# Splits on ScalarE, the cluster assignment in PSUM, and a planner with new numbers

## The chip, the cores and the metric

The kernel runs on one core of a Trainium2 chip. The core has five engines that each take their instructions in order: TensorE (PE, with its weight loads PEld), VectorE (DVE), ScalarE (ACT), GpSimd (POOL) and SyncE (SP, which here issues the DMAs). Time is device microseconds, the median of several runs. The profile is of one execution.

## The reference

Attention over 4 batches and 8 heads, 768 tokens, head size 64, in which a query sees only the keys of its own cluster, and then a soft mixture of experts over the result:

```python
q_n = q / (np.linalg.norm(q, axis=-1, keepdims=True) + 1e-06)   # k_n, c_n alike
q_assign = np.argmax(np.einsum('bhsd,hcd->bhsc', q_n, c_n), axis=-1)   # 16 clusters; k_assign alike
mask = q_assign[:, :, :, None] == k_assign[:, :, None, :]
scores = np.where(mask, scale * np.matmul(q, k.transpose(0, 1, 3, 2)), -1000000000.0)
scores = scores - np.max(scores, axis=-1, keepdims=True)
attn = np.exp(scores)
attn = attn / (np.sum(attn, axis=-1, keepdims=True) + 1e-09)
x = np.matmul(attn, v)          # [3072, 512] once the heads are side by side
logits = x @ phi                # 32 slots, 4 for each of 8 experts
slot_input = softmax(logits, over='tokens').T @ x      # written out in the reference
slot_out[e] = np.maximum(slot_input[e] @ w1[e], 0.0) @ w2[e]
out = softmax(logits, over='slots') @ slot_out
```

## The kernel before

Attention works through 32 heads in 16 pairs. For a pair, TensorE multiplies q and k with the centroids (`sims`), ScalarE scales the result (`sims_out`), TensorE transposes it into a PSUM bank (`assign`), and VectorE finds the first largest of 16 similarities for every token (`assign1` to `assign3`, lines 470 to 490): a maximum, a comparison with it into bfloat16 in SBUF, a multiplication with 16, 15, ... 1, another maximum, and two comparisons that write one-hot rows. `onehot` transposes these, and they become 32 more rows of the operands, so that the score product carries the mask.

For a head, q^T and k^T arrive in `R` (three buffers). `split_hi` (line 512) rounds them to the type of TensorE's faster float32 products into `RH`, `split_lo` (line 515) writes what is left into `RL` (two buffers each). DMAs within SBUF (`place1`, `place2`, `place_mask`, `place3`, line 325) lay the pieces and the mask out as operands. `splitv_hi` (line 543, or 541 on ScalarE) and `splitv_lo` (line 547) split v likewise into float16 (`vx`, two buffers). Pass a (line 560) computes scores in nine steps, each into one of two PSUM banks, and VectorE takes the row maxima of each (`rowmax`, line 568). The maxima go back as a row of the operands (`maxrow`, line 583, and a small DMA). Pass b (line 603) computes the transposed scores for six key tiles into two PSUM buffers; ScalarE takes the exponential of each twice (`expo`, line 609: float32 and float16), GpSimd subtracts one from the other (`elow`, line 613), and pass c (line 625) multiplies both parts with v and accumulates. VectorE divides by the sums (`norm`, lines 637 to 639). Transposes and logits of the finished pair follow, and after eight heads the routing of one batch. The experts come after the last head. Forty pieces of expert weights are loaded during the attention, the others into the buffers that the attention leaves.

In the kernel before, `HI_ACT` puts `split_hi` of heads 0 and 1 on ScalarE and the other 30 on VectorE, and `EARLY` does the same with `splitv_hi`.

The order of all this is made by a planner when the kernel is built (`Plan`). Each operation has an engine, an assumed duration, the buffers that it reads and writes, and a priority from the table `K`; the planner simulates the engines and always takes, of the operations that can start first, the one of the lowest number. What it emits is the fixed order of each engine's instructions; the hardware then only follows it and waits on semaphores. A PSUM bank shared by all small products (`pt`, one buffer: `sims`, `assign`, `onehot`, `maxrow`, `xtrans`, `logits` and the routing) is modelled as a token: `get` takes it, `put` returns it.

Of the kernel before, what the change touches and what calls it, by code (L numbers as in the profile page):

```python
# [19 lines left out]
P = 128  # L20
LOOK = 0.0
HI_ACT = lambda i: i < 2 or i % 2 == HA
HA = 2
MX_ACT = False
WARM0 = 60
WARM1 = (0, 4, 3, 2, 4, 1)   # after the last xtrans, xtrans, logits, dtrans, slotin, comb
EARLY = 2              # heads whose first steps keep off the vector engine


class Plan:  # L30
    """Operations in program order, with the buffers that they read and write; order() lets every
# [15 lines left out]
    def op(self, eng, us, key, t, fn, rd=(), wr=(), get=None, put=None, after=(), xfer=0.0):  # L47
# [16 lines left out]
        self.ops.append((eng, us, t + self.K[key], fn, deps, get, put, xfer, key, t))  # L64
# [12 lines left out]
    def order(self, look=LOOK, banks=1):  # L77
# [9 lines left out]
        dma = tail = 0.0  # L87
        gets, puts = [], {}
# [16 lines left out]
        while len(out) < N:  # L105
# [42 lines left out]
def clustered_attention_then_soft_moe(  # L148
    ctx: ExitStack,
    tc: tile.TileContext,  # L150
    qkT: bass.AP,    # [B, H, 2*D, S]    rows 0:D = q^T, rows D: = k^T
    vt: bass.AP,     # [B, H, 128, S/128, D]
    cent: bass.AP,   # [128, H/2, D]   rows (half, head, q|k, cluster), for every pair of heads
    cbdT: bass.AP,   # [2*D, H, 2*NCL] centroids^T for q and for k, zero elsewhere
    phi2: bass.AP,   # [128, DM/128, NS]
    w1r: bass.AP,    # [2, 4, 128, 4, F]
    w2a: bass.AP,    # [2, 2, 128, 4, F/256, DM/2]   first half of the columns
    w2b: bass.AP,    # [2, 2, 128, 4, F/128, DM/4]   the other two quarters
    out: bass.AP,    # [B*S, DM]
# [4 lines left out]
    NT = S // P                  # token tiles of a head  # L164
    HS = S // 2                  # half of the tokens
# [35 lines left out]
    descb = const.tile([P, NCL], BF16, name="descb")  # L201
# [6 lines left out]
    def consts1():  # L208
        nc.vector.tensor_copy(descb, desc)
# [18 lines left out]
    # of the batches so far, rows (quarter of the tokens, slot):  # L228
    # min of -logits, sum of exp, sum of exp * x
# [7 lines left out]
    # Sixteen chunks of expert weights go through NWB buffers; the last of the  # L237
    # buffers hold tiles of the attention first.
# [5 lines left out]
    # two of them are allocated in parts, which change their type when the weights come  # L244
# [49 lines left out]
    # the last columns of the arenas  # L294
# [6 lines left out]
    swp = cols(ar7, A0 + NCC * NS, P)            # adds up the quarters  # L301
# [236 lines left out]
    def splitv_hi(i):  # L538
        o = VXs[i % 2][:, :, D:2 * D]
        if i < EARLY:  # L540
            nc.scalar.mul(o, V[i % 2], VS)  # L541
        else:
            nc.vector.tensor_scalar_mul(o, V[i % 2], VS)  # L543
# [689 lines left out]
```

## Time and profile before

| | |
|---|---|
| median of 3 runs | 562.71 us (562.12 to 568.84) |
| the profiled execution | span 563.4 us; no other time of its own is given, and the span is 0.7 us above the median |
| DVE busy | 465.5 us, 83% of the span |
| PE busy | 478.6 us, 85% |
| ACT busy | 340.2 us, 60% |
| POOL busy | 345.7 us, 61% |
| DMA, mean | 184 GB/s |

Busy time is the union of an engine's instructions. Matmuls overlap and their ends are modelled, so PE's figure holds some drain time as well. The 83% of DVE is a mean over stages: it is higher during the attention, and low in the last 80 us, in which the experts run.

### The profile page before, as it was taken

The page shows a single profiled execution, that of the slowest core. Times are in us where ns is not written, and L with a number is a line of the kernel's source. Part 1 is how long each engine was busy: PE and PEld are TensorE (multiplying, and loading weights), DVE is VectorE, ACT ScalarE, POOL GpSimd, SP SyncE. Part 2 cuts the span into 40 slices and gives each one's busy share as a digit, 9 for nine tenths or more (in the row PEclk, how much of TensorE's full clock was granted, in tenths as well). Part 3 has the DMA queues.
Part 4 walks back from the last instruction along what each step waited for, and adds up shares of the span by engine and source line. Part 5 has one row for each costly group of instructions (what it writes and reads, how often), then busy time and mean ns, then how long its engine had stood idle before and what let it go on. Part 6 is the DMA issues. An engine that isn't in the chain of part 4 may idle for free.

```text
span 563.4 us, 15227 instructions
## 1 busy us (share of the span) xinstructions
PE 478.6 (85%) x6083; PEld 376.8 (67%) x6083; DVE 465.5 (83%) x786; ACT 340.2 (60%) x494; POOL 345.7 (61%) x255
## 2 busy tenths in 40 slices
PE   8896868789888889789888889887988799899994
PEld 6685657577767667667676667776765678764484
DVE  3799698998989998989899998999899988452253
ACT  4176536676667667667676667676765687830142
POOL 7067465777767657777766578676866598714210
PEclk9999878999999999999999999999999899999998
DMA  8824537346656566676666646665765478999978
GB/s 222 216 70 120 152 98 204 102 130 186 172 142 178 147 154 164 178 177 155 169 168 180 155 125 161 181 176 151 174 175 151 132 204 203 308 311 382 408 248 239
DMA packets 55082, 103.79 MB, mean 184 GB/s; under 512 B 8490, under 2 KB 22372, under 8 KB 55012
## 3 DMA queue, kind: packets, MB, share of 16 engines
q1 hardware_dynamic: 55012, 102.82, 65.2%
q8 instruction: 48, 0.79, 0.6%
q14 instruction: 22, 0.18, 0.1%
HBM read 52.76 MB, written 6.29 MB: 105 GB/s over the span
## 4 chain that ended last, share of the span: by engine, by line
DVE 49%; PE 28%; DMA 12%; issue 5%; SPq 3%; ACT 1%; POOL 0%; DVEq 0%; ACTq 0%; POOLq 0%
DVE mc L568 16%; DMA w<-w 11%; DVE w L515 8%; PE pa L560 6%; PE pc L625 6%; DVE vx L543 5%; PE pb L603 5%; DVE w L512 3%; PE pso L1103 3%; PE ph L1041 2%; SPq L325 2%; DVE w L478 2%; DVE w L488 2%; DVE vx L547 2%; PE po L1124 2%
## 5 line engine op out<-in xcount | busy, mean ns | idle before, releaser
L613 POOL TENSOR_TENSOR w<-w,w 128x768 f16<-128x768 f32 x188 | 322.6, 1737 | 161.1 <-PE pc L625 81.7
L609 ACT ACTIVATE w<-pb 128x768 f32<-128x768 f32 (+1 forms) x384 | 285.0, 815 | 105.0 <-PE pb L603 102.5
L568 DVE TENSOR_REDUCE mc<-pa 128x1 f32<-128x512 f32 (+1 forms) x288 | 187.4, 679 | 17.9 <-PE pa L560 16.7
L560 PE MATMUL pa<-w 128*128 128x512 f32 (+1 forms) x384 | 120.9, 386 | 56.3 <-DVE mc L568 44.1
L603 PE MATMUL pb<-w 128*128 128x512 f32 (+1 forms) x576 | 152.6, 353 | 1.5 <-DMA w<-w 1.4
L625 PE MATMUL pc<-vx,w 128*128 128x65 f16 (+1 forms) x3456 | 123.0, 194 | 3.3 <-DVE w L639 3.0
L560 PEld LDWEIGHTS pa<-w 128*128 128x128 f32 x384 | 61.4, 191 | 89.0 <-DVE mc L568 72.4
L625 PEld LDWEIGHTS <-w 128*128 128x128 f16 x3456 | 112.3, 98 | 11.3 <-DVE w L639 3.9
L603 PEld LDWEIGHTS pb<-w 128*128 128x128 f32 x576 | 105.0, 193 | 18.2 <-issue 1.7
L603 PE MATMUL pb<-w,w 128*128 128x512 f32 x192 | 61.0, 340 | 0.0
L515 DVE TENSOR_TENSOR w<-w,w 128x768 fp32r<-128x768 f32 x30 | 48.9, 1630 | 0.1
L603 PEld LDWEIGHTS pb<-w,w 128*128 128x128 f32 x192 | 36.5, 190 | 7.1 <-DVE w L592 0.3
L543 DVE TENSOR_SCALAR vx<-w 128x384 f16<-128x384 f32 x30 | 35.6, 1185 | 0.0
L512 DVE CAST w<-w 128x768 fp32r<-128x768 f32 x30 | 27.6, 919 | 3.5 <-DMA w<-w 2.8
L462 ACT ACTIVATE w<-pt,crn 128x384 f32<-128x384 f32 x16 | 9.3, 581 | 30.7 <-PE pt L454 30.6
L547 DVE SCALAR_TENSOR_TENSOR vx<-w,vx 128x384 f16<-128x384 f32 x32 | 25.5, 797 | 1.8 <-ACT vx L541 1.7
L992 PE MATMUL pc<-ident 128*128 128x128 f32 x148 | 22.0, 301 | 1.4 <-POOL ident masks.py:199 1.4
L992 PEld LDWEIGHTS pc<-ident 128*128 128x128 f32 x148 | 20.2, 212 | 3.1 <-issue 1.6
L500 ACT ACTIVATE w<-pt,ohsc 128x768 fp32r<-128x768 bf16 x15 | 13.5, 901 | 12.5 <-PE pt L497 12.4
L653 ACT COPY xT<-pt 128x384 f32<-128x384 f32 x30 | 14.6, 488 | 10.0 <-PE pt L648 10.0
L488 DVE TENSOR_TENSOR w<-w,m 128x192 bf16<-128x192 bf16 x32 | 19.4, 645 | 0.3
L478 DVE TENSOR_TENSOR w<-w,descb 128x384 bf16<-128x384 bf16 x16 | 19.0, 1190 | 0.0
(138 smaller groups left out, 379.3 us busy)
## 6 DMA issues: line engine op xcount, KB each, us to landing
w<-w SPq DMA_DIRECT2D x128, 192.0 KB
w<-w SPq DMA_DIRECT2D x188, 96.0 KB
w<-w1r SPq DMA_DIRECT2D x64, 256.0 KB
w<-qkT SPq DMA_DIRECT2D x32, 384.0 KB
w<-w2a SPq DMA_DIRECT2D x32, 256.0 KB
w<-w2b SPq DMA_DIRECT2D x16, 512.0 KB
w<-vt SPq DMA_DIRECT2D x32, 192.0 KB
out<-w SPq DMA_DIRECT2D x24, 256.0 KB
```

What stands on the lines that cost most here:

```text
L488: nc.vector.tensor_tensor(oh[:, :, k, 0:NCL], wv[:, :, k, :], mv[:, :, k].unsqueeze(2).to_broadcast([P, NG // 2, NCL]), op=cmp)
L512: (nc.scalar.copy if HI_ACT(i) else nc.vector.tensor_copy)(RH[i % 2], R[i % 3])
L515: (nc.gpsimd if i < EARLY else nc.vector).tensor_sub(RL[i % 2], R[i % 3], RH[i % 2].bitcast(F32))
L543: nc.vector.tensor_scalar_mul(o, V[i % 2], VS)
L547: nc.vector.scalar_tensor_tensor(vx[:, :, 0:D], V[i % 2], VS, vx[:, :, D:2 * D], op0=ALU.mult, op1=ALU.subtract)
L560: nc.tensor.matmul(pa[:, c0:c0 + w], q1[:, q0:q0 + P], k1[:, k0:k0 + w], start=True, stop=True)
L568: nc.vector.tensor_reduce(hd[i]["mc"][:, 4 * m + c0:4 * m + c1], pa.rearrange("p (n c) -> p n c", n=c1 - c0), axis=AX.X, op=ALU.max, negat ...
L603: nc.tensor.matmul(pbt[j % 2][:, q0:q1], k_[:, kc], q_[:, q0:q1], start=(o == 0), stop=(o == 1))
L609: nc.scalar.activation(dst[:, j % 2, :], pbt[j % 2][:, 0:S], AF.Exp, scale=SCALE)
L613: eng.tensor_tensor(EL[(NT * i + j) % NEL], E32[o % 2][:, j % 2, :], EH[o % (NEH // 2)][:, j % 2, :], op=ALU.subtract)
L625: nc.tensor.matmul(pc[:, t * W:t * W + w], e[:, ts], vx[:, j, r0:r0 + w], start=(j == 0 and t == 0 and o == 0), stop=(j == NT - 1 and o == ...
L992: nc.tensor.matmul(d["pc"][:, 0:P], ident, ident, start=True, stop=True)
```

## The change

- `split_hi` and `splitv_hi` of all 32 heads run on ScalarE.
- `assign1` to `assign3` work in place on the float32 similarities in the PSUM bank; the bfloat16 buffers `eq` and `wt` and the table `descb` go away. The bank `pt` is returned after `assign3`, not after `assign1`.
- The planner gets new durations, a larger latency between engines (0.28, was 0.23), and a notion of a shared port: operations marked `port` (GpSimd's `elow`, `split_lo`, `splitv_lo`, and VectorE's forms of them) are planned so that only one of them runs at a time.
- The table of priorities `K` is replaced by another. Its rows tell nothing by themselves.

On SP's queue the two DMAs of a head's mask (`place_mask`) now stand ahead of `place1`'s for most heads; before, they stood behind them.

`XT_DVE` and `VLO_POOL` are false everywhere, so they change nothing.

```diff
-HI_ACT = lambda i: i < 2 or i % 2 == HA
-HA = 2
+HI_ACT = lambda i: True
+VHI_ACT = lambda i: True
+VLO_POOL = lambda i: False
+XT_DVE = lambda p, u: False
...
-    LAT = 0.23            # from one engine to another
+    LAT = 0.28
...
         def start(n):
             t = ready[n]
+            if self.ops[n][10]:
+                t = max(t, port[0])
...
+            if self.ops[n][10]:
+                port[0] = t + us
...
-    eqwt = cols(ar1, 4 * S + HS, HS).bitcast(BF16)
-    eq = eqwt[:, 0:HS].rearrange("p (g c) -> p g c", c=NCL)
-    wt = eqwt[:, HS:2 * HS].rearrange("p (g c) -> p g c", c=NCL)
...
     K = dict(
...
-        onehot_out=-206.7, split_hi=-74.4, place1=-118.85, split_lo=250.35, place2=-191.1,
...
+        sims_out=494.13, split_hi=-432.68, split_lo=1025.42, splitv_hi=1334.45, splitv_lo=383.03,
...
-        nc.vector.tensor_tensor(eq, pv, mx.unsqueeze(2).to_broadcast([P, NG, NCL]), op=ALU.is_equal)
+        nc.vector.tensor_tensor(pv, pv, mx.unsqueeze(2).to_broadcast([P, NG, NCL]), op=ALU.is_equal)
...
-        nc.vector.tensor_tensor(wt, eq, descb.unsqueeze(1).to_broadcast([P, NG, NCL]),
+        pv = pr[p]["ps"][:, 0:HS].rearrange("p (g c) -> p g c", c=NCL)
+        nc.vector.tensor_tensor(pv, pv, desc.unsqueeze(1).to_broadcast([P, NG, NCL]),
                                 op=ALU.mult)
-        m2 = pr[p]["m2"] = wk1.tile([P, NG], BF16, name="m2")
-        nc.vector.tensor_reduce(m2, wt, axis=AX.X, op=ALU.max)
+        m2 = pr[p]["m2"] = wk1.tile([P, NG], F32, name="m2")
+        nc.vector.tensor_reduce(m2, pv, axis=AX.X, op=ALU.max)
...
-        wv = wt.rearrange("p (g k) c -> p g k c", k=2)
+        wv = pr[p]["ps"][:, 0:HS].rearrange("p (g k c) -> p g k c", k=2, c=NCL)
...
-        if i < EARLY:
+        if VHI_ACT(i):
             nc.scalar.mul(o, V[i % 2], VS)
...
-        op("DVE", 1.06, "assign1", s0, lambda p=p: assign1(p), [], [("eq", p)], put=("assign", p))
-        op("DVE", 0.865, "assign2", s0, lambda p=p: assign2(p), [("eq", p), ("const", 1)], [("eq", p)])
-        op("DVE", 0.54, "assign3", s0, lambda p=p: assign3(p), [("eq", p)], [("oh", p)])
+        op("DVE", 1.06, "assign1", s0, lambda p=p: assign1(p), [], [("eq", p)], after=[plan.writers[("assign", p)][0]])
+        op("DVE", 1.06, "assign2", s0, lambda p=p: assign2(p), [("eq", p), ("const", 1)], [("eq", p)])
+        op("DVE", 0.66, "assign3", s0, lambda p=p: assign3(p), [("eq", p)], [("oh", p)], put=("assign", p))
...
-                    op("DVE", 0.6, f"ra{3 * m + n}", h0, lambda i=i, m=m, n=n: rowmax(i, m, n), [k], [("mc", i)])
+                    op("DVE", 0.635, f"ra{3 * m + n}", h0, lambda i=i, m=m, n=n: rowmax(i, m, n), [k], [("mc", i)])
...
-                op("ACT", 1.38, "x", t, lambda i=i, j=j: expo(i, j), [("pb", n)], [("e32", n), ("eh", n)])
+                op("ACT", 1.46, "x", t, lambda i=i, j=j: expo(i, j), [("pb", n)], [("e32", n), ("eh", n)])
```

The changed file has other line numbers: 480 is `split_hi` there, 483 `split_lo`, 509 and 515 the two halves of v, 429 `sims_out`, 468 `onehot_out`, 440 to 456 the assignment, 536 `rowmax`, 577 the exponentials, 581 `elow`.

VectorE before, around the splits of a head in the middle of the attention (`w_88` holds q and k, `w_89` their halves, `vx_121` the split v, `pa_133` and `pa_134` the banks of pass a):

```order
L512 CAST w_89<-w_88 128x768
L568 TENSOR_REDUCE mc<-pa_133 128x1
L543 TENSOR_SCALAR vx_121<-w_96 128x6x64
L568 TENSOR_REDUCE mc<-pa_134 128x1
L515 TENSOR_TENSOR w_89<-w_88,w_89 128x768
L568 TENSOR_REDUCE mc<-pa_133 128x2
L547 SCALAR_TENSOR_TENSOR vx_121<-w_96,vx_121 128x6x64
```

The same place now (`w_87` holds q and k, `w_88` their halves):

```order
L515 SCALAR_TENSOR_TENSOR vx_120<-w_95,vx_120 128x6x64
L536 TENSOR_REDUCE mc<-pa_132 128x1
L536 TENSOR_REDUCE mc<-pa_133 128x2
L483 TENSOR_TENSOR w_88<-w_87,w_88 128x768
L696 COPY acc<-pt 128x512
```

Two of the four split instructions have left the engine, and the order of the other two is turned round.

VectorE before, the assignment of the eighth pair (the bank is `pt`; the one-hot rows go into `w_89`):

```order
L473 TENSOR_REDUCE mx<-pt 128x24
L474 TENSOR_TENSOR w_88<-pt,mx 128x384
L568 TENSOR_REDUCE mc<-pa_133 128x1
L568 TENSOR_REDUCE mc<-pa_134 128x2
L574 TENSOR_REDUCE nmx<-mc 128x6
L478 TENSOR_TENSOR w_88<-w_88,descb 128x384
L481 TENSOR_REDUCE m_2798<-w_88 128x24
L488 TENSOR_TENSOR w_89<-w_88,m_2798 128x12x16 x2
```

And now:

```order
L440 TENSOR_REDUCE mx<-pt 128x24
L441 TENSOR_TENSOR pt<-pt,mx 128x384
L536 TENSOR_REDUCE mc<-pa_132 128x1
L536 TENSOR_REDUCE mc<-pa_133 128x2
L446 TENSOR_TENSOR pt<-pt,desc 128x384
L449 TENSOR_REDUCE m_2823<-pt 128x24
L456 TENSOR_TENSOR w_88<-pt,m_2823 128x12x16 x2
```

The steps are the same and stand as close together; all but the last now read and write `pt`, and the bank is free only after the last.

ScalarE before, from the scaling of the eighth pair's similarities on (`w_96` and `w_97` are the two exponentials, `pb_131` and `pb_132` the banks of pass b):

```order
L462 ACTIVATE w_88<-pt,crn 128x384
L609 ACTIVATE w_96<-pb_131 128x768
L609 ACTIVATE w_97<-pb_131 128x768
L609 ACTIVATE w_96<-pb_132 128x768
L609 ACTIVATE w_97<-pb_132 128x768
L609 ACTIVATE w_96<-pb_131 128x768
L609 ACTIVATE w_97<-pb_131 128x768
L609 ACTIVATE w_96<-pb_132 128x768
L609 ACTIVATE w_97<-pb_132 128x768
L653 COPY xT_117<-pt 128x384
```

And now (`w_95` and `w_96` are the two exponentials, `pb_130` and `pb_131` the banks):

```order
L429 ACTIVATE w_87<-pt,crn 128x384
L577 ACTIVATE w_95<-pb_130 128x768
L577 ACTIVATE w_96<-pb_130 128x768
L577 ACTIVATE w_95<-pb_131 128x768
L577 ACTIVATE w_96<-pb_131 128x768
L577 ACTIVATE w_95<-pb_130 128x768
L577 ACTIVATE w_96<-pb_130 128x768
L509 ACTIVATE vx_118<-w_95 128x6x64
L468 ACTIVATE w_87<-pt,ohsc 128x768
L480 CAST w_88<-w_87 128x768
L577 ACTIVATE w_95<-pb_131 128x768
L577 ACTIVATE w_96<-pb_131 128x768
```

The splits of v (509) and of q and k (480) stand between exponentials; the exponentials behind them wait if a split waits.

More of the change, by code (lines that the diff above doesn't have):

```diff
@@ L45, in touching, with op @@
         return [o for t in tokens for o in self.touch.get(t, [])]
-    def op(self, eng, us, key, t, fn, rd=(), wr=(), get=None, put=None, after=(), xfer=0.0):
+    def op(self, eng, us, key, t, fn, rd=(), wr=(), get=None, put=None, after=(), xfer=0.0, port=False):
         n = len(self.ops)
@@ L87, in order @@
         dma = tail = 0.0
+        port = [0.0]
         gets, puts = [], {}
@@ L200, in clustered_attention_then_soft_moe @@
                    allow_small_or_imprecise_dtypes=True)
-    descb = const.tile([P, NCL], BF16, name="descb")
     ohsc = const.tile([P, 1], F32, name="ohsc")
@@ new lines, in clustered_attention_then_soft_moe @@
+        load_v=1046.17, load_w=680.22, logits=504.57, maxrow=-2389.55, maxrow_out=358.53,
+        norm=372.77, onehot=-196.58, onehot_out=562.14, p0_assign=1074.92, p0_assign1=-78.81,
+        p0_assign2=1559.02, p0_assign3=-475.83, p0_onehot=-1360.22, p0_onehot_out=905.94,
+        p0_sims=-599.32, p0_sims_out=249.65, p1_assign=-430.46, p1_assign1=1154.32,
+        p1_assign2=-80.5, p1_assign3=-2311.17, p1_load_r=-100.9, p1_onehot=-310.55,
+        p1_onehot_out=560.24, p1_sims=-748.5, p1_sims_out=562.62, place1=-353.32, place2=-7.63,
@@ L652, in xtrans_out @@
         pr[p]["xT", u] = xTs[u]
-        (nc.scalar.copy if apool(p) is None else nc.vector.tensor_copy)(pr[p]["xT", u], pr[p][u][:, 0:HS])
+        (nc.vector.tensor_copy if XT_DVE(p, u) or apool(p) is not None else nc.scalar.copy)(pr[p]["xT", u], pr[p][u][:, 0:HS])
     def logits(p):
@@ L822, in clustered_attention_then_soft_moe @@
             early = i < EARLY
-            op(*(("ACT", 0.75) if HI_ACT(i) else ("DVE", 0.47)), "split_hi", h0, lambda i=i: split_hi(i), [("R", i)], [("rh", i)])
+            op(*(("ACT", 0.76) if HI_ACT(i) else ("DVE", 0.47)), "split_hi", h0, lambda i=i: split_hi(i), [("R", i)], [("rh", i)],
+               port=not HI_ACT(i))
             for k in range(3):
                 op("SP", 0.625, "place1", h0, lambda i=i, k=k: place1(i, k), [("rh", i)], [("q1", i)], xfer=0.55)
-            op(*(("POOL", 1.6) if early else ("DVE", 0.87)), "split_lo", h0, lambda i=i: split_lo(i), [("R", i), ("rh", i)], [("rl", i)])
+            op(*(("POOL", 1.6) if early else ("DVE", 0.87)), "split_lo", h0, lambda i=i: split_lo(i), [("R", i), ("rh", i)], [("rl", i)],
+               port=True)
             op("SP", 0.625, "place2", h0, lambda i=i: place2(i), [("rl", i)], [("q1", i)], xfer=0.27)
@@ L852, in clustered_attention_then_soft_moe @@
             op("SP", 0.45, "load_v", h0, lambda i=i: load_v(i), wr=[("v", i)], xfer=0.55)
-            op(*(("ACT", 0.5) if early else ("DVE", 0.27)), "splitv_hi", h0, lambda i=i: splitv_hi(i), [("v", i)], [("vx", i)])
-            op("DVE", 0.47, "splitv_lo", h0, lambda i=i: splitv_lo(i), [("v", i), ("vx", i)], [("vx", i)])
+            op(*(("ACT", 0.47) if VHI_ACT(i) else ("DVE", 0.27)), "splitv_hi", h0, lambda i=i: splitv_hi(i), [("v", i)], [("vx", i)],
+               port=not VHI_ACT(i))
+            op(*(("POOL", 0.85) if VLO_POOL(i) else ("DVE", 0.47)), "splitv_lo", h0, lambda i=i: splitv_lo(i), [("v", i), ("vx", i)], [("vx", i)],
+               port=True)
             for m in range(NT // 2):
@@ L894, in clustered_attention_then_soft_moe @@
                get=None if alt else ("xtrans", p, u))
-            op("DVE" if alt else "ACT", 0.45 if alt else 0.37, f"xtrans_out{u}", s0, lambda p=p, u=u: xtrans_out(p, u), [("px", 2 * p + u)],
+            op(*(("DVE", 0.48) if alt or XT_DVE(p, u) else ("ACT", 0.41)), f"xtrans_out{u}", s0, lambda p=p, u=u: xtrans_out(p, u), [("px", 2 * p + u)],
                [("xT", 2 * p + u)], put=None if alt else ("xtrans", p, u))
@@ L970, in clustered_attention_then_soft_moe @@
     held = (
-        last("R", 0, S, 3) + last("ohs", 3 * S, S, 1) + last("sT", 4 * S, HS, 1) + last("eq", 4 * S + HS, HS, 1)
+        last("R", 0, S, 3) + last("ohs", 3 * S, S, 1) + last("sT", 4 * S, HS, 1)
         + [(A0, CW - A0, plan.touching(("R", NH - 2), ("R", NH - 1)))],
```

160 lines of the change are left out of this document (59 added, 101 removed).

## The prediction

> **What bounds the kernel now.** I read the page's sums first, then cut the span into stages.
>
> ```profile
> span 563.4 us, 15227 instructions
> PE 478.6 (85%) x6083; PEld 376.8 (67%) x6083; DVE 465.5 (83%) x786; ACT 340.2 (60%) x494; POOL 345.7 (61%) x255
> ```
>
> The sums name no single bound. For stages I took the marks that ScalarE's timeline gives, the scaling of a pair's similarities (`sims_out`), once in a pair:
>
> ```profile
> 105.37 0.58 ACT L462 ACTIVATE w<-pt,crn 128x384 f32<-128x384 f32 x1 [3.09 <-PE pt L454]
> ...
> 399.20 0.58 ACT L462 ACTIVATE w<-pt,crn 128x384 f32<-128x384 f32 x1 [1.28 <-PE pt L454]
> ```
>
> Between these two lie ten pairs, 293.8 us or 29.4 a pair. The windows view (columns: length, busy us of PE, PEld, DVE, ACT, POOL with counts, granted clock, DMA share, GB/s) with cuts there and at 483.5, just before the last split of v ends:
>
> ```profile
> 0.00:105.40 105.40, 84.86 (x844) 67.65 (x844) 83.62 (x139) 54.07 (x76) 58.75 (x52) 0.94 0.57 147
> 105.40:399.20 293.80, 249.85 (x3279) 201.33 (x3280) 273.05 (x454) 201.18 (x287) 205.80 (x121) 1.00 0.62 163
> 399.20:483.50 84.30, 74.82 (x982) 61.34 (x982) 76.79 (x131) 60.20 (x88) 60.90 (x37) 0.98 0.65 174
> 483.50:563.40 79.90, 69.06 (x982) 46.45 (x980) 32.06 (x66) 24.71 (x45) 20.26 (x48) 0.97 0.91 323
> ```
>
> In the ten pairs VectorE is busy 273.05 of 293.8 us (93%), 20.75 idle; PE has 85%, ScalarE and GpSimd 68 to 70%. The waits say the same: PE's products of pass a wait for row maxima, and ScalarE for PE.
>
> ```profile
> ACT w L609 <- PE pb L603: 102.5, 95, 7.5
> PEld pa L560 <- DVE mc L568: 72.4, 85, 5.6
> PE pa L560 <- DVE mc L568: 44.1, 45, 5.5
> ```
>
> So VectorE sets the pace until about 483; the last 80 us have little of it and the DMA engines at 91%. Next, what fills VectorE. The source view gives shortest, median and longest duration (ns) of the instructions that the change touches, and of GpSimd's subtraction:
>
> ```profile
> L512 DVE CAST w<-w x30: 537/654/1849, 21.1 to 459.3; 128x768 fp32r<-128x768 f32 x30
> L543 DVE TENSOR_SCALAR vx<-w x30: 348/1264/1807, 52.7 to 482.4; 128x384 f16<-128x384 f32 x30
> L515 DVE TENSOR_TENSOR w<-w,w x30: 940/1796/2410, 21.7 to 462.3; 128x768 fp32r<-128x768 f32 x30
> L478 DVE TENSOR_TENSOR w<-w,descb x16: 348/1323/1807, 12.6 to 439.9; 128x384 bf16<-128x384 bf16 x16
> L488 DVE TENSOR_TENSOR w<-w,m x32: 343/419/1796, 13.7 to 443.6; 128x192 bf16<-128x192 bf16 x32
> L613 POOL TENSOR_TENSOR w<-w,w x188: 1639/1654/2371, 33.6 to 494.1; 128x768 f16<-128x768 f32 x188
> ```
>
> One instruction of one shape takes 348 ns or 1807. The spread is about one GpSimd subtraction long. The timeline shows why:
>
> ```profile
> 222.62 1.65 POOL L613 TENSOR_TENSOR w<-w,w 128x768 f16<-128x768 f32 x1 [0.20 <-POOL w L613]
> 223.47 1.22 DVE L512 CAST w<-w 128x768 fp32r<-128x768 f32 x1 [1.01 <-DMA w<-w]
> ```
>
> GpSimd ends at 224.27, and VectorE's cast ends 0.42 us later, about its short duration: it counts as busy while it waits for GpSimd. This excess is what the change can reach.
>
> **The change part by part.** In the ten pairs (line groups of that window: count, busy us, mean ns):
>
> ```profile
> L515 DVE TENSOR_TENSOR w<-w,w 128x768 fp32r<-128x768 f32 x19 | 34.5, 1816 | 0.0
> L543 DVE TENSOR_SCALAR vx<-w 128x384 f16<-128x384 f32 x21 | 26.6, 1265 | 0.0
> L512 DVE CAST w<-w 128x768 fp32r<-128x768 f32 x19 | 18.4, 968 | 2.3 <-DMA w<-w 1.6 <-issue 0.7
> L547 DVE SCALAR_TENSOR_TENSOR vx<-w,vx 128x384 f16<-128x384 f32 x20 | 15.3, 765 | 0.0
> L478 DVE TENSOR_TENSOR w<-w,descb 128x384 bf16<-128x384 bf16 x10 | 12.2, 1223 | 0.0
> L488 DVE TENSOR_TENSOR w<-w,m 128x192 bf16<-128x192 bf16 x20 | 11.2, 597 | 0.1
> L474 DVE TENSOR_TENSOR w<-pt,mx 128x384 bf16<-128x384 f32 x10 | 5.6, 557 | 0.3
> L743 DVE TENSOR_TENSOR call<-pt,cm 128x192 f32<-128x192 f32 x2 | 0.7, 358 | 0.1
> ```
>
> *Splits.* VectorE loses L512 and L543: 18.4 + 26.6 = 45.0 us. ScalarE gains them. It ran both for the first two heads:
>
> ```profile
> L512 ACT CAST w<-w 128x768 fp32r<-128x768 f32 x2 | 1.7, 832 | 1.0 <-DMA w<-qkT 1.0
> L541 ACT ACTIVATE vx<-w 128x384 f16<-128x384 f32 x2 | 1.1, 528 | 2.1 <-DMA w<-vt 2.1
> ```
>
> 20 × 0.832 + 20 × 0.528 = 27.2 us, so ScalarE goes from 201.2 to 228.4. These rows stand before GpSimd's first subtraction at 33.6; that GpSimd stretches ScalarE isn't shown anywhere, so I take none. Behind a split in ScalarE's order stand exponentials; for these wait PE's next pass b (its two banks) and GpSimd.
>
> [...]
>
> *Assignment.* The multiplication goes from 1223 ns to that of a float32 operation on the bank, L474's 557 (write into PSUM isn't shown; 348, the short bfloat16 form, to the present 1223 bound it): 12.2 − 5.6 = 6.6 us gone. The two comparisons of 192 go from 597 to L743's 358 (343 to 597): 11.2 − 7.2 = 4.0. The other steps keep their length. [...] The bank stays taken for the multiplication, a maximum and two comparisons longer, some 2 us a pair. PE's order after the assignment's transposes has pass a, b and c until the one-hot transposes, which need that result anyway, so I cost it at nothing; without that cover it is 2 us × 10 = 20.
>
> *What stays.* L515 and L547 (34.5 + 15.3 us) still meet GpSimd. At their shortest they'd be some 29 us, at the longest 19 × 2.41 + 20 × 1.88, far more. The planner now keeps them apart in its plan, but GpSimd will be busy more of the time; I leave them as they are.
>
> *Sum for VectorE:* 273.05 − 45.0 − 6.6 − 4.0 = 217.4, under ScalarE's 228.4. GpSimd stays near 206. PE's 249.85 is then the largest, but holds drain time. The first row is the timeline's, with the modelled end, the second the chain's, from start to the next start:
>
> ```profile
> 202.03 1.28 PE L625 MATMUL pc<-vx,w 128*128 128x65 f16 x36
> ...
> 37.86 1.12 PE pc L625 x36
> ```
>
> Sixty such groups in ten pairs hold 60 × 0.16 = 9.6 us of it: 240 is needed. If the new bound reaches VectorE's present 93%, the stage takes 240/0.93 = 258 by PE, 228.4/0.93 = 246 by ScalarE. PE's other products end in drains too, so I take 254: **40 us less**, 25.4 a pair. New orders of pass a, b and c cost nothing by themselves: the same products, in runs as long. On SP's queue the mask's DMAs now stand ahead of `place1`'s; pass a needs both, so I cost this at nothing while `onehot_out` comes on time, and at the wait for it where not (this is in the fourth rival).
>
> *Outside.* L543 by stage, in the windows view of that line alone (length, busy, count):
>
> ```profile
> 0.00:105.40 105.40, 3.37 (x4) 0.94 0.57 147
> 105.40:399.20 293.80, 24.77 (x21) 1.00 0.62 163
> 399.20:483.50 84.30, 7.42 (x7) 0.98 0.65 174
> ```
>
> The last stage of attention has 30% of the middle's cost, so 30% of 40 = 12 less; it empties towards its end, so 9. The first has 14%: 5 (from 5 to 15, as VectorE is also late there). After 483.5 nothing that the change shortens remains: 0. Sum: 40 + 9 + 5 = **54**; 563.4 − 54 = 509.4, and 0.7 less on the median's scale: 509.
>
> **The rivals.** Outside the ten pairs each goes by the same ratio, 54/40 = 1.35.
>
> *The wait moves.* If the excess of L512 and L543 is a wait for GpSimd that the next two-input instruction inherits, VectorE sheds only the short durations: 19 × 0.537 + 21 × 0.348 = 17.5, less 2.4 for the slower assignment: 258 busy, with 20.75 idle 279, 15 less, × 1.35 = 20: 543. [...] For it: GpSimd gets denser. Against: L568, most of what follows, stays at its length next to GpSimd.
>
> *PE paces.* If the recorded 249.85 is needed in full and the idle remains: 270.6, 23 less, × 1.35 = 31: 532. For it: 85% busy now. Against: its idle time is nearly all before L560, for VectorE.
>
> *Slower: splits block ScalarE.* A split needs its load, and the buffer that the DMAs of two heads earlier have read. Such DMAs show in the chain:
>
> ```profile
> 218.95 4.34 DMA w<-w
> ...
> 231.19 3.69 DMA w<-w
> ```
>
> If each of the 20 `split_hi` stands 4 us in front of the exponentials, ScalarE takes 228.4 + 80 = 308, with 10 to 20 idle 318 to 328: 30 more, × 1.35 = 40: 603. It breaks even where 228.4 + 20 w reaches 273, w = 2.2 us. Against: L512 lost 2.3 us in all to waits in ten pairs.
>
> *Nothing gained.* The new order costs what the durations save (a bank held when a transpose needs it, maxima late in ScalarE's or SP's queue): 563 ± 11.
>
> **How the numbers follow.** Forecast 0.57, at its own range 487 to 525: the low end has ScalarE's 228.4 with 9 idle, 57 × 1.35 = 76 less, 487. PE paces 0.20; the wait moves 0.12; nothing 0.07; slower 0.04. The range 487 to 543 holds the first three but for some of the third. Faster by over 2% (under 551.5, about what a measurement can tell): 0.57 + 0.20 + 0.10 = 0.87; within 0.09, with a part of "the wait moves"; slower 0.04.
>
> **What would show it.** Right: the pair's marks about 25 us apart; casts of 0.83 and 0.53 us on ScalarE; VectorE under 90% in the middle; the multiplication near 0.56 us with little spread. Wrong: `split_hi` on ScalarE behind waits for DMA; L483 and L515 (the new lines) longer than 1.8 and 0.8 us in the mean; pass a waiting for maxima as much as now.

## The result and the profile after

The changed kernel takes 526.47 us (median of 4 runs, 517.55 to 527.86) beside 562.91 (562.12 to 568.84) before: 36 us less. The ratio is 0.923, 95% interval 0.9121 to 0.9339; it leaves out runs over 1.5% slower than the fastest of their kernel, and since three of these four runs take 525 to 528 us and one 517.55, it says more gain than the medians do, 43 us. The forecast of 509 was 17 us too low by the median and 11 by the ratio; the measured time lies inside the range of 487 to 543.

The profiled run took 525.13 us. The page's sums:

```profile
span 523.4 us, 15341 instructions
PE 474.8 (91%) x6083; PEld 379.3 (72%) x6083; DVE 368.6 (70%) x725; ACT 368.7 (70%) x554; POOL 330.7 (63%) x255
```

VectorE has 97 us less than before, ScalarE 28 more, and TensorE's share is now the largest. The same marks as in the prediction (the scaling of a pair's similarities, line 429 now) bound the ten pairs:

```profile
89.09 0.59 ACT L429 ACTIVATE w<-pt,crn 128x384 f32<-128x384 f32 x1
...
362.94 0.57 ACT L429 ACTIVATE w<-pt,crn 128x384 f32<-128x384 f32 x1
```

The windows view of what lies ahead of the ten pairs and of these (length, busy us of PE, PEld, DVE, ACT, POOL with counts, granted clock, DMA share, GB/s):

```profile
0.00:89.10 89.10, 78.36 (x847) 64.92 (x848) 69.65 (x134) 59.32 (x86) 55.41 (x52) 1.00 0.65 174
89.10:362.90 273.80, 253.04 (x3293) 206.84 (x3292) 208.68 (x412) 219.85 (x328) 197.35 (x121) 0.97 0.65 175
```

The ten pairs went from 293.8 to 273.8 us (20 less, 40 forecast), what lies ahead of them from 105.4 to 89.1 (16 less, 5 forecast). Behind them a common mark is the experts' first product, which starts at 510.2 us before and at 470.7 now: up to it the rest of the attention goes from 111.0 to 107.8 (3 less, 9 forecast), and from it to the end the experts go from 53.2 to 52.7. These parts add up to the 40 us by which the two profiled spans differ; the medians differ by 36. VectorE is no bound any more: 208.7 of 273.8. TensorE comes nearest to filling the ten pairs, with 253.0 of 273.8 (92%), but its granted clock is 0.97 where it was 1.00. The groups of the ten pairs (count, busy us, mean ns, then the idle time before them and who ended it) show what became of the operations:

```profile
L480 ACT CAST w<-w 128x768 fp32r<-128x768 f32 x21 | 17.5, 833 | 26.7 <-DMA w<-w 19.6 <-issue 3.9 <-DVE mc L536 1.4
L509 ACT ACTIVATE vx<-w 128x384 f16<-128x384 f32 x20 | 11.0, 552 | 0.0
L483 DVE TENSOR_TENSOR w<-w,w 128x768 fp32r<-128x768 f32 x20 | 20.2, 1009 | 12.7 <-ACT w L480 12.7
L515 DVE SCALAR_TENSOR_TENSOR vx<-w,vx 128x384 f16<-128x384 f32 x20 | 13.7, 683 | 0.0
L446 DVE TENSOR_TENSOR pt<-pt,desc 128x384 f32<-128x384 f32 x10 | 5.6, 556 | 0.0
L456 DVE TENSOR_TENSOR w<-pt,m 128x192 bf16<-128x192 f32 x20 | 6.2, 352 | 0.3
```

The first row has what is new: ScalarE stands 26.7 us in front of `split_hi`, 19.6 of them until a DMA within SBUF has ended. The waits of the same stage (who waits for whom: us, times, longest) show whom this hits. TensorE's weight loads (PEld) and its products (PE) often stand at the same time, so their rows must not be added (after the change their sum would be more than PE's whole idle time); PE's row is time in which no product runs. First before, in its ten pairs, then after:

```profile
PEld pa L560 <- DVE mc L568: 47.2, 59, 2.0
PE pa L560 <- DVE mc L568: 27.0, 34, 1.5
```

```profile
PEld pb L571 <- ACT w L577: 25.3, 21, 3.9
PE pb L571 <- ACT w L577: 19.1, 16, 3.6
PEld pa L528 <- DVE mc L536: 6.4, 13, 0.8
```

Of PE's 44.0 us of idle time before (293.8 − 249.85), 27.0 were waits for row maxima. Now it has 20.8 us (273.8 − 253.04), none of it for row maxima and 19.1 for the exponentials, in front of which the splits stand. So the stage lost 23.2 us of idle time and gained 3.2 us of busy time, at a lower clock: 20.0 us less.

One such wait in the timeline (start, length, engine, line, idle time before):

```profile
150.71 2.41 SPq L327 DMA_DIRECT2D w<-w  x4
...
157.34 0.49 PE L616 MATMUL pt<-ident,w 128*128 128x128 f32 x3
...
158.26 0.83 ACT L480 CAST w<-w 128x768 fp32r<-128x768 f32 x1 [2.95 <-DMA w<-w]
...
160.56 1.65 PE L571 MATMUL pb<-w 128*128 128x512 f32 x4 [2.72 <-ACT w L577]
...
162.43 0.63 PE L571 MATMUL pb<-w 128*128 128x512 f32 x1
...
167.24 0.39 PE L571 MATMUL pb<-w 128*128 128x512 f32 x1
```

The four DMAs of `place3` are issued by 153.1 and read the halves; the split of the head after next needs that buffer, waits for a DMA within SBUF and starts at 158.26, some 5 us after that. ScalarE has stood 2.95 us, and TensorE 2.72. After that a product of 512 columns takes 0.63 us at first and 0.39 from 167 on. Windows around it:

```profile
155.00:160.00 5.00, 2.83 (x48) 2.35 (x46) 2.83 (x6) 2.05 (x4) 1.20 (x1) 0.97 0.64 189
160.00:165.00 5.00, 4.45 (x16) 3.96 (x16) 2.60 (x5) 3.79 (x6) 4.32 (x3) 0.50 0.26 62
```

The granted clock is 0.50 for those 5 us. So here a wait of 3 us cost its length and some of the time after.

### The profile page after: what moved, and what is told of

Its sections match the earlier page's. It is cut to its first block, busy times and chain, and to the rows that moved or that the text cites. A ratio compares the mean times of both kernels' runs of the same rounds, so it can differ in the third digit from the quotient of the medians.

```text
span 523.4 us, 15341 instructions
## 1 busy us (share of the span) xinstructions
PE 474.8 (91%) x6083; PEld 379.3 (72%) x6083; DVE 368.6 (70%) x725; ACT 368.7 (70%) x554; POOL 330.7 (63%) x255
## 4 chain that ended last, share of the span: by engine, by line
PE 29%; DMA 8%; SPq 5%; ACT 5%; DVE 4%; issue 2%; ACTq 0%; DVEq 0%
PE pb L571 7%; DMA w<-w 6%; PE pc L593 6%; ACT w L577 4%; SPq L327 3%; PE pa L528 3%; PE pso L1075 3%; PE ph L1013 3%; DMA w<-w1r 2%; PE po L1096 2%; DVE mc L536 1%; SPq L930 1%; PE pt L421 1%; DVE vx L515 1%; DVE w L483 1%
## 5 line engine op out<-in xcount | busy, mean ns | idle before, releaser
L581 POOL TENSOR_TENSOR w<-w,w 128x768 f16<-128x768 f32 x188 | 307.9, 1659 | 136.5 <-ACT w L577 104.7
L571 PE MATMUL pb<-w 128*128 128x512 f32 (+1 forms) x576 | 155.3, 357 | 27.4 <-ACT w L577 23.5
L571 PEld LDWEIGHTS pb<-w 128*128 128x128 f32 x576 | 105.7, 193 | 56.5 <-ACT w L577 32.8
L528 PE MATMUL pa<-w 128*128 128x256 f32 (+1 forms) x384 | 123.5, 383 | 7.7 <-DVE mc L536 3.6
L528 PEld LDWEIGHTS pa<-w 128*128 128x128 f32 x384 | 64.8, 196 | 24.1 <-DVE mc L536 14.9
L480 ACT CAST w<-w 128x768 fp32r<-128x768 f32 x32 | 26.7, 835 | 39.7 <-DMA w<-w 24.3
L483 DVE TENSOR_TENSOR w<-w,w 128x768 fp32r<-128x768 f32 x30 | 32.0, 1066 | 14.9 <-ACT w L480 14.9
L515 DVE SCALAR_TENSOR_TENSOR vx<-w,vx 128x384 f16<-128x384 f32 x32 | 24.5, 766 | 0.0
L607 DVE TENSOR_TENSOR w<-pc,z 128x384 f32<-128x384 f32 (+1 forms) x33 | 18.0, 545 | 1.1
L509 ACT ACTIVATE vx<-w 128x384 f16<-128x384 f32 x32 | 17.6, 550 | 1.2 <-DMA w<-vt 1.2
L1075 PE MATMUL pso<-w,hT 128*32 128x128 f32 (+1 forms) x384 | 16.4, 311 | 0.0
L616 PE MATMUL pt<-ident,w 128*128 128x128 f32 x90 | 15.9, 288 | 0.0
```

The lines of the kernel that those rows point to most:

```text
L480: (nc.scalar.copy if HI_ACT(i) else nc.vector.tensor_copy)(RH[i % 2], R[i % 3])
L483: (nc.gpsimd if i < EARLY else nc.vector).tensor_sub(RL[i % 2], R[i % 3], RH[i % 2].bitcast(F32))
L515: (nc.gpsimd if VLO_POOL(i) else nc.vector).scalar_tensor_tensor(vx[:, :, 0:D], V[i % 2], VS, vx[:, :, D:2 * D], op0=ALU.mult, op1=ALU.sub ...
L528: nc.tensor.matmul(pa[:, c0:c0 + w], q1[:, q0:q0 + P], k1[:, k0:k0 + w], start=True, stop=True)
L571: nc.tensor.matmul(pbt[j % 2][:, q0:q1], k_[:, kc], q_[:, q0:q1], start=(o == 0), stop=(o == 1))
L581: eng.tensor_tensor(EL[(NT * i + j) % NEL], E32[o % 2][:, j % 2, :], EH[o % (NEH // 2)][:, j % 2, :], op=ALU.subtract)
```

## The experiments

Every kernel is timed beside the kernel before on its own chip. That one's medians were 562.1 beside the first four kernels, 563.5 beside the next four and 564.0 beside the last four. A distance from the changed kernel is given by medians. By the ratios the changed kernel stands some 7 us lower (0.923 × 562.91 = 519.6), so by them a slower kernel loses some 7 us more than is said, and a faster one gains so much less. What is read from a profile holds for that one run.

### A third buffer for the halves

Theory A: the gain that is missing is `split_hi`'s wait for its buffer. Theory B: TensorE paces. With a third buffer (in columns that later hold expert weights, so for heads up to 20) the split waits for reads of three heads before, not two. The order of all instructions is that of the changed kernel.

```diff
+    RH.append(wbuf[NPRE - 1][:, 0:S].bitcast(F32R))
+    RHN = lambda i: i % 3 if i < 21 else i % 2
...
-        (nc.scalar.copy if HI_ACT(i) else nc.vector.tensor_copy)(RH[i % 2], R[i % 3])
+        (nc.scalar.copy if HI_ACT(i) else nc.vector.tensor_copy)(RH[RHN(i)], R[i % 3])
...
```

> The changed kernel with a third buffer for the high halves of q and k for the first 21 heads (the third lies where a piece of expert weights is loaded only from head 22 on); the order of all instructions is unchanged. Theory A, ScalarE is blocked: in the changed kernel the split of a head stands in front of exponentials and waits for the DMAs that still read the half of two heads earlier, 39.7 us in all, some 23 us of it for heads up to 20; behind it PE stops and then runs at a lower clock. With a third buffer those waits go: 10 to 20 us off the changed kernel's 525, so 505 to 515, and idle before the split near 15 us. Theory B, PE paces (92% busy in the ten pairs): the time stays within 5 us of 525, and PE's waits for ScalarE turn into waits for something else. Theory C, the DMA queue paces: the split then waits for its load, or pass a for the first placing DMAs, and nothing is gained.

Measured: 510.5 us (504.84 to 513.27), ratio 0.9045 (0.8977 to 0.9113). The ten pairs take 257.7 us in place of 273.8. Windows and waits of these pairs (lines are two higher: 482 is `split_hi`):

```profile
91.30:349.00 257.70, 246.42 (x3283) 202.66 (x3281) 210.67 (x412) 218.61 (x328) 200.92 (x121) 0.99 0.68 185
```

```profile
PEld pa L530 <- DVE mc L538: 15.8, 24, 2.3
PE pa L530 <- DVE mc L538: 5.9, 7, 2.1
PEld pb L573 <- ACT w L579: 5.3, 6, 1.8
ACT w L482 <- DMA w<-w: 4.1, 3, 1.8
PE pb L573 <- ACT w L579: 3.3, 4, 1.6
```

The split's wait for DMAs falls from 19.6 to 4.1 us. PE's wait for the exponentials falls from 19.1 to 3.3, and 5.9 us of waiting for row maxima come back. Of the 16.1 us, 9.5 are idle time of PE (20.8 to 11.3) and 6.6 its busy time (253.0 to 246.4), while the clock rises from 0.97 to 0.99. Theory A holds.

Since 2 to 3% depend on it and the runs of both kernels scatter, both ran once more on one chip, six times each.

> The changed kernel itself, on the chip and in the call of the three others, so that differences of one to three per cent can be told. Every theory: 520 to 528 us.

> The changed kernel with a third buffer for the halves of heads up to 20, as in the first experiment, beside the changed kernel. Theory A (the splits' wait for the buffers of two heads before is the largest loss of the changed kernel): 505 to 515 us, at least 10 us below the changed kernel. Rival (the two earlier figures came from two chips): less than 6 us below it.

Measured: 527.79 us (516.16 to 529.25) and 514.66 (512.46 to 523.0; ratio to before 0.912, 0.9067 to 0.9173). The medians are 13 us apart, as theory A has it; the lowest of the two are only 4 apart, which is the rival's "less than 6". The ten pairs of the two profiled runs are 6.6 us apart (272.1 and 265.5). The sign is the same on both chips; the size, 4 to 16 us, isn't settled.

### The split one key tile later

The other way to take the wait from the exponentials: the same buffers, but each `split_hi` from head 4 on stands behind one more pair of exponentials in ScalarE's order. The rest of the order is kept.

```diff
...
+            if self.ops[n][8].split("_")[-1] == "x":
+                for h in held:
+                    h[1] -= 1
+                act += [h[0] for h in held if h[1] == 0]
...
```

> The changed kernel with each split of q and k from head 4 on moved on ScalarE behind the next pair of exponentials (1.5 us later); all other engines keep their order. Theory A: each wait shrinks by up to 1.5 us, 8 to 15 us off 525: 510 to 517, unless pass a then waits for the placing DMAs, which would show as PE waiting for DMA ahead of pass a. Theory B: within 5 us of 525. Theory C: the loads and placings come later by 1.5 us a head, so the time stays or grows by up to 20.

Measured: 520.74 us (519.69 to 527.51), ratio 0.9255 (0.9211 to 0.9298): next to nothing beside the changed kernel, out of theory A's range and in theory B's. Waits over the whole run (lines are 38 higher):

```profile
PEld pa L566 <- DVE mc L574: 53.7, 57, 2.4
PE pa L566 <- DVE mc L574: 31.6, 25, 2.2
DVE w L521 <- ACT w L518: 19.1, 23, 1.8
ACT w L518 <- DMA w<-w: 3.5, 3, 1.3
```

The split's wait is gone (3.5 us), but `split_lo` on VectorE waits for the later split (19.1 us), and PE waits 31.6 us for the row maxima that stand behind it there (3.6 in the changed kernel's whole run). Of the two ways, the one that only moves the wait to another queue gains nothing.

### More work for ScalarE, more for TensorE

To see which engine paces the changed kernel, two engines got about 20 us more each: every `splitv_hi` twice (32 × 0.55 = 17.6 us), and one quarter product of pass b in each key tile twice, the first result being overwritten.

```diff
             nc.scalar.mul(o, V[i % 2], VS)
+            nc.scalar.mul(o, V[i % 2], VS)
```

```diff
+                if o == 0 and q0 == 512:
+                    nc.tensor.matmul(pbt[j % 2][:, q0:q1], k_[:, kc], q_[:, q0:q1], start=True, stop=True)
```

> The changed kernel with the high half of v computed twice on ScalarE (same result), 32 more instructions of 0.55 us, 17.6 us of ScalarE time in the same places of the order. Theory A, ScalarE is on the path: 10 to 18 us more than 525. Theory B, PE paces and ScalarE has slack: at most 5 more.

> The changed kernel with the first product of 256 columns of each tile of pass b computed twice on PE (the second overwrites the first, same result): 192 more products of some 0.11 us by the spacing in runs, 20 us of PE time. Theory B, PE paces: 18 to 25 us more than 525. Theory A: PE still has its waits for ScalarE to fill, 5 to 12 more.

Measured: 530.35 us (521.48 to 535.59) with ScalarE's work, some 4 over the changed kernel and within the scatter, so the times settle nothing. The profiled run (521.48) has 9.5 us more of ScalarE in its ten pairs, and these take 272.3 us, no longer than the changed kernel's 273.8: ScalarE's own time isn't what paces them there. With TensorE's work 525.28 us (520.84 to 532.55), ratio 0.9385 (0.9306 to 0.9464): for 20 us of work nothing by the medians, 3 to 5 us by the lowest runs and some 9 by the ratios, whose intervals overlap. The ten pairs:

```profile
90.10:361.25 271.15, 259.39 (x3416) 214.94 (x3415) 209.26 (x412) 220.43 (x329) 197.78 (x121) 1.00 0.65 176
```

The stage is no longer than before. PE's idle time is 11.8 us in place of 20.8, so a part of the added products stands where it waited. Its busy time is only 6.3 us more for 120 products of some 0.11 us (13 us, by the spacing in the expectation): the clock is 1.00, and over the whole run pass a's products take 374 ns in the mean, 383 in the changed kernel. Theory B, that the 20 us show whole, falls for the changed kernel.

With the third buffer TensorE is busier (246.4 of 257.7 us, 96%), so the same products were added there.

> The kernel with a third buffer for the halves, and on top the 192 repeated quarter products of pass b that cost the changed kernel nothing (it adds products whose results are overwritten). Theory B2 (with the wait for the buffer gone TensorE paces: 98 per cent busy from 200 to 300 us at full clock): the 20 us of work show nearly whole, 522 to 532 us. Rival (something else still paces, and TensorE follows): up to 515 us.

Measured: 517.16 us (509.47 to 521.27), ratio 0.9096 (0.8997 to 0.9195). Beside 510.5 and 514.66 without the products, on two other chips, this is 2.5 to 6.7 us for 20; the expectation had 522 to 532 by the theory and up to 515 by the rival, so it lies between them. In the profiled run PE is idle for 6.2 us of the ten pairs' 264.2. TensorE is the pace there at most in part. What else is, stays open.

### Which part of the change earns the gain

Three kernels undo or do one part and keep the emitted order. First the splits of heads 2 to 31 back on VectorE, at ScalarE's places:

```diff
-        (nc.scalar.copy if HI_ACT(i) else nc.vector.tensor_copy)(RH[i % 2], R[i % 3])
+        (nc.scalar.copy if i < 2 else nc.vector.tensor_copy)(RH[i % 2], R[i % 3])
...
-        if VHI_ACT(i):
+        if i < 2:
```

> The changed kernel with its planned order kept to the instruction, but split_hi and splitv_hi of heads 2 to 31 executed by VectorE, each at the place in the order at which ScalarE's now stands. Theory A (the gain is VectorE's time, and the splits are most of it): VectorE gets about 45 us back in the ten pairs (18.4 + 26.6, the rows of before) and some 65 us in all, ScalarE loses 28.5 there; 550 to 580 us, and the row maxima become the wait of pass a again (over 60 us in the rows of PE's waits for L536, 18.5 now). Rival P (the new order of the planner earned the gain, wherever the splits run): 526 to 540 us.

Measured: 589.82 us (589.37 to 593.42), ratio 1.049 (1.0426 to 1.0554): 63 us above the changed kernel, more than expected, and slower than before. Groups and waits of the whole run:

```profile
L511 DVE TENSOR_SCALAR vx<-w 128x384 f16<-128x384 f32 x30 | 39.3, 1309 | 0.0
L480 DVE CAST w<-w 128x768 fp32r<-128x768 f32 x30 | 32.9, 1098 | 3.0 <-DMA w<-w1r 2.2 <-DMA w<-w 0.8
```

```profile
PEld pa L528 <- DVE mc L536: 67.3, 73, 2.3
PE pa L528 <- DVE mc L536: 46.6, 40, 2.1
```

PE waits 46.6 us for row maxima again (44.1 before). Not all of the loss is VectorE's time: in the ten pairs, 322.3 us long, it's busy for 271.1 (84%), and the granted clock is 0.90. Without the splits on ScalarE the new order, the assignment in PSUM included, is 26 us slower than the kernel before.

Next the assignment back in SBUF, with its bfloat16 buffers:

```diff
...
-        nc.vector.tensor_tensor(pv, pv, mx.unsqueeze(2).to_broadcast([P, NG, NCL]), op=ALU.is_equal)
+        nc.vector.tensor_tensor(eq, pv, mx.unsqueeze(2).to_broadcast([P, NG, NCL]), op=ALU.is_equal)
...
-        wv = pr[p]["ps"][:, 0:HS].rearrange("p (g k c) -> p g k c", k=2, c=NCL)
+        wv = wt.rearrange("p (g k) c -> p g k c", k=2)
```

> The changed kernel with its planned order kept, but the assignment goes through the two bfloat16 buffers in SBUF as before (the PSUM bank is still given back after assign3). Theory A: VectorE has 3.53 us of assignment a pair in place of 2.38, so 11.5 us more in the ten pairs and 18 in all; VectorE is not full there (208.7 of 273.8 us), so a part of it shows: 528 to 538 us, with the multiplication again over 1000 ns. Rival Q (the assignment in PSUM was worth nothing or less, since the bank is held longer anyway): 522 to 528 us.

Measured: 540.31 us (539.35 to 546.03), ratio 0.9618 (0.9542 to 0.9694): 14 us above the changed kernel, a little more than theory A's range. Shortest, median and longest duration of its multiplication and its last comparisons, and behind them the same two of the changed kernel:

```profile
L449 DVE TENSOR_TENSOR w<-w,descb x16: 347/440/1649, 14.7 to 412.7; 128x384 bf16<-128x384 bf16 x16
L459 DVE TENSOR_TENSOR w<-w,m x32: 345/1307/1804, 15.8 to 415.1; 128x192 bf16<-128x192 bf16 x32
```

```profile
L446 DVE TENSOR_TENSOR pt<-pt,desc x16: 556/556/567, 11.1 to 400.1; 128x384 f32<-128x384 f32 x16
L456 DVE TENSOR_TENSOR w<-pt,m x32: 347/352/359, 12.4 to 401.6; 128x192 bf16<-128x192 f32 x32
```

This time it's mostly not the multiplication that is long (the expectation said so) but the two comparisons behind it: the medians are 440 and 1307 ns. With their similarities in PSUM neither is long, 556 to 567 and 347 to 359 ns, also beside GpSimd: in the changed kernel two comparisons from 186.00 us on take 0.62 us together, while it subtracts from 185.36 to 188.63. VectorE has 21 us more in the ten pairs (229.8, not 208.7), and yet they take only 277.0 us, not 273.8. Most of the 14 us are lost ahead of them: they begin at 99.8 us, not 89.1. The granted clock of this run is 0.98 in the ten pairs and 0.966 over the whole.

Third the splits alone, in the old order, on ScalarE at VectorE's places:

```diff
-        (nc.scalar.copy if HI_ACT(i) else nc.vector.tensor_copy)(RH[i % 2], R[i % 3])
+        nc.scalar.copy(RH[i % 2], R[i % 3])
...
-        if i < EARLY:
+        if True:
```

> The kernel before with its planned order kept to the instruction, but all split_hi and splitv_hi executed by ScalarE, each where VectorE's stood. Nothing else of the change. Theory A: VectorE loses 45 us of its 273 in the ten pairs and what is left paces as in the changed kernel; without the assignment's 11 us and with an order that was not made for it, 525 to 545 us. Rival P (it needs the new order: in the old one the splits stand in ScalarE's queue at places that block the exponentials, or wait for the halves' buffers as in the changed kernel and longer): 550 us or more.

Measured: 542.2 us (538.29 to 543.13), ratio 0.9617 (0.9553 to 0.9681), in theory A's range: 21 us of gain without any new number. Its ten pairs (101.72 to 377.60) take 275.9 us, so the splits alone bring 17.9 of the 20.0 us that the whole change gains in this stage:

```profile
101.72:377.60 275.88, 249.85 (x3279) 203.20 (x3280) 233.50 (x411) 220.11 (x325) 200.02 (x121) 0.99 0.67 173
```

What the change gains beyond them lies mostly ahead of the ten pairs, which begin at 101.7 us here and at 89.1 in the changed kernel. The groups of the whole run:

```profile
L512 ACT CAST w<-w 128x768 fp32r<-128x768 f32 x32 | 26.6, 835 | 3.5 <-DMA w<-w 2.8 <-DVE mc L568 0.7
L515 DVE TENSOR_TENSOR w<-w,w 128x768 fp32r<-128x768 f32 x30 | 42.5, 1415 | 10.5 <-ACT w L512 9.0 <-DMA w<-w 1.2
L547 DVE SCALAR_TENSOR_TENSOR vx<-w,vx 128x384 f16<-128x384 f32 x32 | 29.8, 931 | 2.6 <-ACT vx L541 2.6
```

The same row of the changed kernel's page:

```profile
L480 ACT CAST w<-w 128x768 fp32r<-128x768 f32 x32 | 26.7, 835 | 39.7 <-DMA w<-w 24.3
```

In the old order `split_hi` loses 3.5 us to waits, in the new one 39.7: moving it to ScalarE doesn't by itself make it wait; its place in the new order does.

### The planner's part

The changed kernel planned again without the port rule, and the kernel before with both moves but the old numbers. Both have orders of their own.

```diff
-            if self.ops[n][10]:
-                t = max(t, port[0])
```

> The changed kernel, planned again without the rule that only one operation marked as a user of the port may run at a time; durations, latency and table as in the change, so the order of all engines differs. Theory A (the rule keeps VectorE's split_lo off GpSimd's elow, and this is why its wait did not grow when the other waiting instructions had left): the mean of split_lo goes from 0.96 to 1.3 us or more and that of splitv_lo from 0.68 to 0.85 or more, some 10 to 20 us more of VectorE's time, and 526 to 545 us. Rival (they are short for another reason, the rule is idle): both means within 0.1 us of the changed kernel's.

> The kernel before with both moves (all splits on ScalarE, the assignment in place in PSUM with the bank held until assign3), planned with the old durations, latency and table. Theory A (the moves earn the gain, the new numbers only keep it): splits alone gave 542.2 us in the old order, the assignment saved 14 in the new one; 525 to 545 us. Rival P (without the new table the plan falls apart as it did with the splits on VectorE in the new order, 589.8 us): above 550 us.

Without the rule: 543.15 us (541.47 to 547.12), ratio 0.9633 (0.9577 to 0.969), as theory A had it. The two remaining splits there:

```profile
L481 DVE TENSOR_TENSOR w<-w,w 128x768 fp32r<-128x768 f32 x30 | 40.5, 1351 | 2.7 <-ACT w L478 2.4
L513 DVE SCALAR_TENSOR_TENSOR vx<-w,vx 128x384 f16<-128x384 f32 x32 | 32.9, 1028 | 1.6 <-ACT vx L507 1.6
```

In its timeline VectorE's split starts while GpSimd subtracts and ends after it; in the changed kernel's it stands between two subtractions:

```profile
199.04 3.26 POOL L579 TENSOR_TENSOR w<-w,w 128x768 f16<-128x768 f32 x2 [0.60 <-ACT w L575]
201.45 1.66 DVE L481 TENSOR_TENSOR w<-w,w 128x768 fp32r<-128x768 f32 x1
```

```profile
202.53 1.65 POOL L581 TENSOR_TENSOR w<-w,w 128x768 f16<-128x768 f32 x1 [0.45 <-POOL w L581]
204.20 0.96 DVE L483 TENSOR_TENSOR w<-w,w 128x768 fp32r<-128x768 f32 x1
206.19 8.12 POOL L581 TENSOR_TENSOR w<-w,w 128x768 f16<-128x768 f32 x5 [2.00 <-ACT w L577]
```

In the changed kernel's whole run the means of the two are 1066 and 766 ns. The order of everything else differs too, so the 16.7 us aren't shown to be the rule's; what the rows show is that with it the two splits are shorter in the mean, and that here the one beside a subtraction takes 1.66 us and the one between two 0.96.

Both moves with the old numbers: 554.3 us (548.29 to 556.95), ratio 0.9749 (0.9672 to 0.9827), outside theory A's range and in the rival's, and by the interval not clearly over 2% faster than before. Its two remaining splits are long as well:

```profile
L548 DVE SCALAR_TENSOR_TENSOR vx<-w,vx 128x384 f16<-128x384 f32 x32 | 38.9, 1215 | 1.5 <-ACT vx L542 1.4
L516 DVE TENSOR_TENSOR w<-w,w 128x768 fp32r<-128x768 f32 x30 | 37.6, 1254 | 2.3 <-ACT w L513 2.3
```

That is 76.5 us of VectorE for what takes 56.5 in the changed kernel's whole run (32.0 + 24.5). So the two moves with the old numbers give 9 to 10 us by the medians and 14 by the ratio, and the new numbers the other 27 to 29. They don't add up by parts: splits alone gave 21 in the old order, which was made for another kernel. Why the old numbers do worse with both moves than with the splits alone in the kept order isn't settled; the planning itself differs between the two.

## Why the prediction was right, and where it missed

The measured 526.47 us lie inside the range, but just above the part of it that the forecast took for its own mechanism (487 to 525), among the times of its rivals. That the total came within 17 us is in part luck: the ten pairs gained half of what was forecast, and the first stage three times as much.

**VectorE's bound.** Right. Taking nothing but the two splits away in the old order gained 21 us, and putting them back in the new order cost 63, not all of it VectorE's time. The counted loss was 273.05 − 217.4 = 55.6 us in the ten pairs; 64.4 were measured.

**Prices on ScalarE and in PSUM.** Right: 833 and 552 ns beside 832 and 528 forecast, 556 beside 557, 352 beside 358. At its shortest the multiplication takes 347 ns in bfloat16 in SBUF and 556 in float32 on the bank; by that alone the move would have lost time, and yet with the assignment in SBUF the kernel is 14 us slower. What the move was worth was mis-sized. I took the comparisons' 597 ns of before as the price that goes; in the new order they cost 1284 in the mean of the whole run when they stay in SBUF (645 before), and the multiplication 610 (1190 before): there the long durations fall on the other instruction. The first stage felt it most; why that one isn't shown.

**The bank held longer, at nothing.** Right: in the ten pairs TensorE's only waits for the assignment's new steps are these two.

```profile
PEld pa L528 <- DVE pt L446: 0.2, 1, 0.2
PEld L465 <- DVE w L456: 0.2, 1, 0.2
```

**"I leave them as they are" (L515 and L547).** Wrong to the good: 49.8 us in the ten pairs became 33.9. I had mentioned the planner's rule and given it no price; without it their means in the whole run are 1351 and 1028 ns, with it 1066 and 766. The comparison of the assignment has a like spread where its inputs lie in SBUF: it takes 345 to 1804 ns with both there, and 347 to 359 with one of them in PSUM.

**"The wait moves" (543).** It didn't, and the means of the instructions that could have inherited it show that: `split_lo` went from 1816 to 1009 ns in the ten pairs, `splitv_lo` from 765 to 683. But it wasn't far off: without the port rule these are longer by 0.26 to 0.29 us each. That this kernel takes 543 us too is no proof, since its whole order differs. The sum's 2.4 us for a slower assignment are the differences of the shortest durations (348 to 557 ns ten times, 343 to 358 twenty times), and no run shows them as a loss: with the assignment back in SBUF VectorE had 21 us more in the ten pairs.

**"PE paces" (532).** Nearest in time, and its mechanism isn't borne out: it takes TensorE's work to be needed in full, and 20 us of added products cost the changed kernel nothing by the medians and some 9 us by the ratios. The prediction's own argument against it was too strong as well: of PE's 44.0 us of idle time before, 36.6 lay ahead of L560, and only 27.0 were waits for row maxima.

**The stage of 254.** This is the step that failed. The sum took an engine's load over VectorE's share of 93%, and priced the splits on ScalarE at their durations, with nothing for their waits. It had 240 us of TensorE's work and 14 beside it; the profile has 253.0 busy, with the drains that the sum took off and with products at a granted clock of 0.50 (160 to 165 us), and 20.8 idle. The fourth rival, "splits block ScalarE", had the cause, a split that waits for DMAs two heads back, but I gave it 0.04 by the row of L512 on VectorE, 2.3 us of waiting in ten pairs. That row was true of the old order: on ScalarE in the old order they wait 3.5 us in all. In the new order they wait 26.7 us in ten pairs, 1.3 us a split. The rival's break-even of 2.2 us asked the wrong engine, too. ScalarE's 219.9 + 26.7 = 246.6 are well within 273.8. The price came through TensorE, which waits for the exponentials behind the split (19.1 us of PE's idle time) and, where the trace was followed, then had a granted clock of 0.50 for 5 us. With the wait taken away the ten pairs took 257.7 us on one chip, near the 254 of the sum; on another, the profiled run had 265.5, at a granted clock of 0.960 over the whole run.

**Outside the ten pairs.** The first 105 us gained 16 (forecast 5, with up to 15 named). With the splits back on VectorE the ten pairs begin at 95.6 us, with the assignment back in SBUF at 99.8; the splits alone in the old order begin them at 101.7, 3.7 earlier than before. So both moves seem to act there, together with the new order, but these are single profiles, and the kernel with the third buffer began its ten pairs at 91.3 in one and at 96.7 in another. The rest of the attention gained 3, not 9: the split's buffer may be short there as well, but no run had a third one for its heads, so this isn't shown.

## What to carry to other kernels

An instruction's waits in a trace belong to its place in the order, not to the instruction: the same `split_hi` on ScalarE lost 3.5 us in one order and 39.7 in the other. When a planner is given new numbers, ask of every moved step which buffer it needs, when the DMAs that read that buffer end, and who stands behind it in the new queue. Price such a wait on the engine that is behind it, not on the one that waits. And where VectorE works beside GpSimd, an operand in PSUM (comparisons of 347 to 359 ns, not 345 to 1804), or an order that keeps the two apart (0.96 us for a split, not 1.66), can be worth more than a format that is faster alone (347 ns, not 556).

## What the runs showed that was not expected

- A gap of 2.7 us in TensorE's work (157.8 to 160.56) was followed by a granted clock of 0.50 over the next 5 us, and products of 512 columns took 0.63 in place of 0.39 us.
- More products came with a higher clock: 0.97 in the ten pairs of the changed kernel, 1.00 with 120 products more in them, at nearly the same length of the stage (273.8 and 271.2 us). Over whole runs the clock was 0.956 to 0.982 without them and 0.980 to 0.993 with them.
